# Layer norm, memory-recurrent attention and a squared-ReLU feed-forward layer on one core: loads put in another order, feed-forward slots and stores moved

## The chip, the cores and the metric

The kernel runs on one core of one Trainium2 chip. The core has TensorE (PE; its weight loads are shown apart as PEld), VectorE (DVE), ScalarE (ACT), GpSimd (POOL) and SyncE (SP, which issues DMAs), and 16 DMA engines that all issuing queues share. The metric is the device time of one execution in microseconds (us), the median of several runs. A profile shows one execution; its span goes from the first instruction to the last.

## What is computed

The input is 2048 rows of width 640. `A` is a recurrent attention: 64 segments of 32 rows, each with 8 memory rows in front; the first 8 output rows of one segment are the memory of the next, so the 64 steps run one after the other. `B` is a feed-forward layer of width 1728.

```python
# A: per segment, h = [mem (8 rows); layernorm(x)[segment] (32 rows)]
q, k, v = h @ Wq, h @ Wk, h @ Wv              # 32 heads of 128
p = softmax(where(mask, q @ k.T * 128**-0.5, -1e9))
o = (p @ v) @ Wo                              # 40 rows of 640
mem, out_rows = o[:8], o[8:]                  # mem goes to the next segment
# whole
h  = x + A(layernorm(x))
h2 = h + relu(layernorm(h) @ w1 + b1)**2 @ w2 + b2
```

## The kernel before

All tensors are bf16 and sums are f32 in PSUM. The q, k, v weights (`wq`, `wk`, `wv`: 5 chunks of 128 rows by 4096 columns each) and `wo` (32 heads of 128 by 640) stay in SBUF. Since the width is cut into 4 groups of 160 = 128 + 32, the fifth chunk of each weight is gathered from 4 blocks of 32 rows: a DMA from DRAM to DRAM collects them in `w4s` (called the relay here, issued by ACT) and a second DMA brings them in.

Work goes in 16 batches of 128 rows, each of 4 steps (one step is one segment; `step`, L396). A step multiplies the 8 memory rows and the first 24 rows of its segment by `wq`, `wk`, `wv` (each two halves of 20 matmuls, `half`, `pass_units`), turns q and k by transposes (`turn`), makes scores (`pss`), exponentials, sums (`pz`), the product with v (`po`), and the output projection `pw` of 128 small matmuls. `wo_out` casts it to `o`; `mem_to_hT` turns the first 8 rows of `o` into the memory of the next step. The last 8 rows of each segment (tail) don't feed the memory, so they are computed for the four segments of a batch together: `tail_units` spreads their q, k, v passes, `wo_tail_units` their projection (`psw`) over the steps of the batch before or after. Every step stores 24 rows of `o` to `a_rows` in DRAM (4 DMAs, L501), the tail of a batch another 16 DMAs (L276).

The feed-forward layer of batch b-1 runs inside the steps of batch b, one slot (`ff_slot`) at two places a step: the first after the k passes (tag `pv3`), the second behind `pz` (tag `pv0`). A slot p of 8 does two blocks of w1 (`psf`, 10 matmuls), the two blocks of w2 that belong to slot p-1 (`acc`, 4 matmuls), and ACT's relu and POOL's square for the next. After its matmuls each slot issues on SP the loads of w1 for slot p+1 and w2 for slot p (`ff_load1`, `ff_load2`: two DMAs each, single-buffered `w1c`, `w2c`); w1 is read from `w1d`, a copy of w1 in DRAM that POOL's queue lays out after batch 0 (L589, L591). Before slot 0 come `ff_rows` (reload of x and `a_rows`), `ff_stats` (sum, mean, variance; inverse root by Newton steps on POOL in `ln_root`), `ff_apply` (`hn`) and `ff_turn` (transposes `pth`, `hnT`).

In the last step `last_loads` brings the whole of w1 and w2 into the place of `wq` (`fw`); after the last step come the tail projection of batch 15, the rest of batch 14's slots and the whole feed-forward layer of batch 15.

The order on PE, ACT, DVE and POOL is that of the program (`manual_schedule`); SP is left to the scheduler. The lists in `sl` hold what is put at a place of a step: q (after the q passes), k (after the k passes), v, d (after the second slot), w0 (before `wo_out`), w (end). `pre` and `mid` are the units ahead of and behind `po`, `post` those around `mem_to_hT`.

Of the kernel before, what the change touches and what calls it, by code (L numbers as in the profile page):

```python
# [18 lines left out]
def kernel(  # L19
# [55 lines left out]
    w1d = dram.tile([FC, 128, DC, 128], BF16)  # L75
# [44 lines left out]

    def ln_apply(dst, src, mv, rstd):
        nc.vector.tensor_scalar(out=dst, in0=src, scalar1=mv[:, 0:1], scalar2=rstd[:],  # L122
                                op0=ALU.subtract, op1=ALU.mult)
# [7 lines left out]
    with tc.tile_pool(name="wts", bufs=1) as wts, tc.tile_pool(name="s1", bufs=1) as s1, \  # L131
            tc.tile_pool(name="s2", bufs=2) as s2, tc.tile_pool(name="s4", bufs=4) as s4, \
# [11 lines left out]
        def load_x(b):  # L144
            xt = s1.tile([128, D], BF16, tag="xt", name="xt")
# [8 lines left out]
        for wi, src in enumerate((A_Wq, A_Wk, A_Wv)):  # L154
            nc.scalar.dma_start(out=w4s[wi].rearrange("(g r) f -> g r f", g=G),
                                in_=src.rearrange("(g q) h e -> g q (h e)", g=G)[:, 128:DG, :])
        for wi, (w, src) in enumerate(((wq, A_Wq), (wk, A_Wk), (wv, A_Wv))):
            w2d = src.rearrange("d h e -> d (h e)")
            for c in range(4):
                nc.sync.dma_start(out=w[:, c, :], in_=w2d[c * DG:c * DG + 128, :])  # L160
            nc.sync.dma_start(out=w[:, 4, :], in_=w4s[wi])
        wov = A_Wo.rearrange("h e d -> e h d")
        for j in range(4):
            (nc.sync if j % 2 else nc.scalar).dma_start(out=wo[:, j * 8:(j + 1) * 8, :], in_=wov[:, j * 8:(j + 1) * 8, :])
# [6 lines left out]
        nc.vector.tensor_copy(out=b1f[:], in_=b1b[:])  # L171
# [6 lines left out]
        def ln_b(b):  # L178
# [4 lines left out]
            roots[b] = (mv, ln_root(s1, mv))  # L183
# [77 lines left out]

        def wo_tail_units(b):
# [3 lines left out]
            def unit(k):  # L266
                def f():
# [3 lines left out]
                    if k == 7:  # L271
                        ot = wo_out(st["ps"])
                        for g in range(G):
                            for sp in range(4):
                                r0 = b * 128 + sp * SEG + HD
                                nc.sync.dma_start(out=a_rows[r0:r0 + TL, g * DG:(g + 1) * DG],  # L276
                                                  in_=ot[32 * g + sp * TL:32 * g + (sp + 1) * TL, :])
# [17 lines left out]

        def ff_load1(p):
            for fc in (2 * p, 2 * p + 1):
                if room:
                    w1q.append(room["w1"][:, :, fc * 128:fc * 128 + fs_of(fc)])
                    continue  # L300
                t = s2.tile([128, DC, 128], BF16, tag="w1c", name="w1c")
                nc.sync.dma_start(out=t[:, :, 0:fs_of(fc)], in_=w1d[fc][:, :, 0:fs_of(fc)])
                w1q.append(t)

        def ff_load2(p):
            for fc in (2 * p, 2 * p + 1):
                if room:
                    w2q.append(room["w2"][:, fc, :])
                    continue
                t = s2.tile([128, D], BF16, tag="w2c", name="w2c")  # L310
                fs = fs_of(fc)
                nc.sync.dma_start(out=t[0:fs], in_=B_w2[fc * 128:fc * 128 + fs, :])
                if fs < 128:
                    nc.sync.dma_start(out=t[fs:fs + 1], in_=B_b2.rearrange("(o d) -> o d", o=1))
                w2q.append(t)

        def ff_rows(b):
# [3 lines left out]
            nc.sync.dma_start(out=a_[:], in_=a_rows[b * 128:(b + 1) * 128, :])  # L321
            fst[b] = {"a": a_, "h": h_}

        def ff_stats(b):
# [3 lines left out]
            nc.vector.tensor_tensor(out=f["h"][:], in0=f["a"][:], in1=f["h"][:], op=ALU.add)  # L328
            for j in range(2):
                ln_stats(st, j, f["h"])  # L330
            nc.vector.bn_aggr(out=mv[:], in_=st[:])
            f["mv"], f["r"] = mv, ln_root(s1, mv)
# [15 lines left out]
        def ff_slot(b, p, tag):  # L348
            f = fst[b]
            f1 = []  # L350
            if p < NP:
                ps = psum_v.tile([128, 4, 128], F32, tag=tag, name="psf")
                for j in range(2):
                    fc = 2 * p + j
                    fs = fs_of(fc)
                    w1c = w1q.pop(0)
                    for c in range(DC):
                        nc.tensor.matmul(ps[0:fs, j, :], lhsT=w1c[:, c, 0:fs], rhs=f["hnT"][:, c, :], start=(c == 0),  # L358
                                         stop=(c == DC - 1))
                ff_load1((p + 1) % NP)  # L360
            if p > 0:
                for j in range(2):
# [3 lines left out]
                    w2c = w2q.pop(0)  # L366
                    for hf in range(2):
                        if fc == 0:
                            f["acc", hf] = psum_v.tile([128, 512], F32, tag="acc%d" % hf, name="acc%d" % hf)
                        nc.tensor.matmul(f["acc", hf][:, 0:320], lhsT=t1[0:k, :], rhs=w2c[0:k, hf * 320:(hf + 1) * 320],  # L370
                                         start=(fc == 0), stop=(fc == FC - 1))
            if p < NP:
                ff_load2(p)
                for j in range(2):
# [3 lines left out]
                    t1 = s4.tile([128, 128], BF16, tag="f1", name="f1")  # L378
# [7 lines left out]
            if p == NP:  # L386
# [6 lines left out]
                run_ff(tag)  # L393

        ffq = []

        def run_ff(tag):
            if ffq:
                ffq.pop(0)(tag)

        def step(s, first, pre, mid, post, slots):
# [21 lines left out]
            run(first[2])  # L423
            run(slots.get("k", ()))
            run_ff("pv3")
            turn(qr, qT[:, :, :, 0:SEG], "act", psum_v, "pv0")
            turn(kr, kT[:], "dve", psum_v, "pv1")
            pv = [psum.tile([128, 512], F32, tag="mm", name="ps%d" % n) for n in range(1)]
# [42 lines left out]
            run_ff("pv0")  # L471
# [166 lines left out]
```

## Time and profile before

| what | us |
|---|---|
| median of 5 runs (1294.22 to 1300.98) | 1297.53 |
| the profiled execution | 1297.53 |
| its span, first to last instruction | 1295.5 |
| mean granted TensorE clock, as a share | 0.981 |
| DMA: 112.55 MB in 97577 packets, mean | 87 GB/s |

In a row of a timeline stand the start, the time taken, engine, line, operation, out<-in, shapes and the count; in brackets the idle time of the engine before it and what ended it. "issue" means that nothing in the profile shows what the engine waited for. A row that stands for several instructions has their common span. A row of waits has the engine and line, what was waited for, us in total, how often, and the longest.

### The profile page before, as it was taken

The numbers are of one execution on the slowest core, as the hardware profiler recorded it, in microseconds if no ns is written. First come the engines' busy times: TensorE is split into PE (matmuls) and PEld (weight loads), VectorE is DVE, ScalarE is ACT, GpSimd is POOL, SyncE is SP. The second block draws the span as 40 slices with busy tenths as digits, with TensorE's granted clock in tenths as the row PEclk, the third lists the DMA queues.
The fourth block names the chain that finished last, engine by engine and source line by source line (L and its number), as shares of the span: only waits on it lengthen the run. The fifth ranks groups of instructions, "written<-read, shape, count | busy, mean of one in ns | idle before, by whom it ended". The sixth has DMA issues, their size and how long they took to land. (4 is left out here: it accounts for less than half of the span.)

```text
span 1295.5 us, 68304 instructions
## 1 busy us (share of the span) xinstructions
PE 1085.8 (84%) x31488; PEld 707.8 (55%) x31488; DVE 464.4 (36%) x987; ACT 414.2 (32%) x848; POOL 304.4 (23%) x981
## 2 busy tenths in 40 slices
PE   0057878999999999989999899899998999899865
PEld 0025545656566665656565565656565665656553
DVE  0003333344343434344433434343433434343411
ACT  0012323334333333333333333333333333333312
POOL 3001132222222222222222222222222222222213
PEclk9999989999999999999999999999999999999977
DMA  7840031223223232223222232223222232222250
GB/s 302 329 151 5 6 94 31 77 77 91 63 66 89 75 86 63 78 71 91 68 78 72 76 91 60 71 76 92 77 71 68 77 92 71 61 68 86 77 182 17
DMA packets 97577, 112.55 MB, mean 87 GB/s; under 512 B 30732, under 2 KB 94123, under 8 KB 95323
## 3 DMA queue, kind: packets, MB, share of 16 engines
q1 hardware_dynamic: 94078, 100.19, 25.2%
q8 instruction: 246, 4.03, 1.2%
q10 hardware_dynamic: 2140, 5.77, 1.2%
q0 software_dynamic: 1072, 2.23, 0.6%
q14 instruction: 41, 0.33, 0.1%
HBM read 102.88 MB, written 10.60 MB: 88 GB/s over the span
## 5 line engine op out<-in xcount | busy, mean ns | idle before, releaser
L208 PEld LDWEIGHTS <-hT 128*32 128x32 bf16 x7680 | 205.3, 97 | 183.3 <-DVE hT L287 7.9
L227 PE MATMUL pw<-wo,oT 128*32 128x160 bf16 x8192 | 167.5, 237 | 45.9 <-issue 42.4
L227 PEld LDWEIGHTS <-oT 128*32 128x32 bf16 x8192 | 148.1, 99 | 69.4 <-issue 50.5
L208 PE MATMUL ps<-wv,hT 128*32 128x512 bf16 x2560 | 163.5, 383 | 0.0
L381 POOL TENSOR_TENSOR f<-ffr 128x128 bf16<-128x128 bf16 x224 | 84.3, 396 | 327.0 <-ACT ffr L379 275.5
L208 PE MATMUL ps<-wq,hT 128*32 128x512 bf16 x2560 | 153.3, 385 | 6.4 <-DVE hT L287 6.2
L208 PE MATMUL ps<-wk,hT 128*32 128x512 bf16 x2560 | 149.8, 379 | 0.0
L129 DVE CAST vr<-ps 128x512 bf16<-128x512 f32 x128 | 88.5, 692 | 72.1 <-PE ps L208 68.7
L379 ACT ACTIVATE ffr<-psf,b1f 128x128 bf16<-128x128 f32 x224 | 68.9, 358 | 91.8 <-PE psf L358 90.0
L129 DVE CAST qr<-ps 128x512 bf16<-128x512 f32 x64 | 44.3, 692 | 139.8 <-PE ps L208 139.8
L232 DVE CAST o<-pw 128x160 bf16<-128x160 f32 x64 | 20.8, 325 | 183.0 <-PE pw L227 179.5
L127 ACT COPY qT<-pt 128x1024 bf16<-128x1024 bf16 x64 | 64.8, 1012 | 58.2 <-PE pt L220 58.2
L358 PE MATMUL psf<-hnT,w1c 128*128 128x128 bf16 (+1 forms) x1020 | 76.0, 220 | 8.6 <-DMA w1c<-w1d 8.6
L451 POOL TENSOR_TENSOR p<-p,mask_t 128x128 bf16<-128x128 bf16 x64 | 27.4, 429 | 223.8 <-ACT p L444 223.8
L129 DVE CAST oT<-po 128x320 bf16<-128x320 f32 x128 | 56.9, 486 | 64.2 <-PE po L486 54.0
L127 ACT CAST qr<-ps 128x512 bf16<-128x512 f32 x64 | 37.5, 586 | 122.1 <-PE ps L208 122.1
L127 ACT CAST tq<-pst 128x512 bf16<-128x512 f32 x32 | 19.0, 592 | 176.9 <-PE pst L208 176.9
L358 PEld LDWEIGHTS <-w1c 128*128 128x128 bf16 (+1 forms) x1020 | 60.6, 99 | 25.5 <-issue 11.5
L370 PE MATMUL acc<-w2c,f 128*128 128x320 bf16 x404 | 72.6, 301 | 1.9 <-DMA w2c<-in_B_w_dram 1.9
L127 ACT CAST oT<-po 128x320 bf16<-128x320 f32 x128 | 48.2, 429 | 68.7 <-PE po L486 68.7
L127 ACT CAST kr<-ps 128x512 bf16<-128x512 f32 x64 | 37.5, 586 | 100.3 <-PE ps L208 100.3
L467 POOL TENSOR_TENSOR pn<-p,rk 128x128 bf16<-128x128 bf16 x64 | 42.7, 667 | 107.1 <-issue 80.8
(97 smaller groups left out, 1373.9 us busy)
## 6 DMA issues: line engine op xcount, KB each, us to landing
w1c<-w1d SPq DMA_DIRECT2D x190, 160.0 KB
w2c<-in_B_w_dram SPq DMA_DIRECT2D x188, 160.0 KB
wq<-in_A_Wq_dram SPq DMA_DIRECT2D x4, 1024.0 KB
wk<-in_A_Wk_dram SPq DMA_DIRECT2D x4, 1024.0 KB
wv<-in_A_Wv_dram SPq DMA_DIRECT2D x4, 1024.0 KB
a_rows<-o SPq DMA_DIRECT2D x256, 7.5 KB
a_rows<-o SPq DMA_DIRECT2D x256, 2.5 KB
xt<-in_A_x_dram SPq DMA_DIRECT2D x16, 160.0 KB
```

Of the source, the lines that this page charges most:

```text
L127: nc.scalar.copy(out=out_, in_=in_)
L129: nc.vector.tensor_copy(out=out_, in_=in_)
L208: nc.tensor.matmul(ps[32 * g:32 * g + 32, :], lhsT=lhs(c), rhs=w[:, c, g * EG + n * 512:g * EG + (n + 1) * 512], start=(c == 0), stop=(c = ...
L227: nc.tensor.matmul(ps[32 * g:32 * g + 32, 0:DG], lhsT=lhs(h), rhs=wo[:, h, g * DG:(g + 1) * DG], start=(h == 0), stop=(h == H - 1))
L232: nc.vector.tensor_copy(out=o[:], in_=ps[:, 0:DG])
L358: nc.tensor.matmul(ps[0:fs, j, :], lhsT=w1c[:, c, 0:fs], rhs=f["hnT"][:, c, :], start=(c == 0), stop=(c == DC - 1))
L370: nc.tensor.matmul(f["acc", hf][:, 0:320], lhsT=t1[0:k, :], rhs=w2c[0:k, hf * 320:(hf + 1) * 320], start=(fc == 0), stop=(fc == FC - 1))
L379: nc.scalar.activation(out=r[0:fs], in_=ps[0:fs, j, :], func=ACT.Relu, bias=b1f[0:fs, fc:fc + 1], scale=1.0)
L381: nc.gpsimd.tensor_tensor(out=t1[0:fs], in0=r[0:fs], in1=r[0:fs], op=ALU.mult)
L451: nc.gpsimd.tensor_tensor(out=p[:, :, NQ:NC], in0=p[:, :, NQ:NC], in1=mask_t[:, sp].unsqueeze(1).to_broadcast([128, HG, M + TL]), op=ALU.mult)
L467: nc.gpsimd.tensor_tensor(out=pn[:, :, NQ:NC].rearrange("p i (a q) -> p i a q", q=M), in0=p[:, :, NQ:NC].rearrange("p i (a q) -> p i a q", ...
```

## The change

- The start: SP is put under the program's order as well. The relays go from ACT's queue to SP's, one ahead of each weight, with 16 rows as the outermost dimension in place of 4 groups; all of `wo` goes to SP; the second batch's x is loaded at the start into another buffer; the first two inverse roots are made on ACT (`ln_root_act`: logarithm, then exponential); the cast of the bias `b1f` moves to batch 1. In step 0 the first v tail passes stand behind the turns.
- w1's copy in DRAM is laid out by pairs of blocks, `[FC // 2, 128, DC, 256]`, one DMA on SP in each of steps 0 to 6. A slot then has one DMA for w1 and one for w2.
- The loads of a slot are put in a list `later`. Those of the first slot go out at once, those of the second (`hold`) behind the first store of `o`, or at the end of the step's stores.
- The 16 tail stores are queued and issued in two lots of 8: behind the stores of step 0 of a batch, and at v of step 1. `ff_rows` moves to d of step 1.
- `ff_apply` moves to k of step 2, `ff_turn` to a new place f ahead of `mem_to_hT` in step 2, and the 8 slots to steps 3, 0, 1, 2. The last slot no longer calls the next item.
- The end: `last_loads` stands after the first slot, loads pairs in the order of use, and builds a selection matrix `sel`. The last rows of batch 15 no longer go through `a_rows`: eight matmuls with `sel` put them into PSUM (`pa`) and `ff_stats` adds them. Its statistics come ahead of batch 14's last slots, and the roots of batches 14 and 15 are made on ACT.
- `f1` has three buffers in place of four.

```diff
-    w1d = dram.tile([FC, 128, DC, 128], BF16)
+    w1d = dram.tile([FC // 2, 128, DC, 256], BF16)
...
+    def ln_root_act(pool, mv):
+        rstd = pool.tile([128, 1], F32, tag="lnrs", name="lnrs")
+        nc.scalar.activation(out=rstd[:], in_=mv[:, 1:2], func=ACT.Ln, bias=eps_t[:])
+        nc.scalar.activation(out=rstd[:], in_=rstd[:], func=ACT.Exp, scale=-0.5)
+        return rstd
...
-                                                        mybir.EngineType.DVE, mybir.EngineType.Pool}))
+                                                        mybir.EngineType.DVE, mybir.EngineType.Pool,
+                                                        mybir.EngineType.SP}))
...
         load_x(0)
+        load_x(1)
...
-        for wi, src in enumerate((A_Wq, A_Wk, A_Wv)):
-            nc.scalar.dma_start(out=w4s[wi].rearrange("(g r) f -> g r f", g=G),
-                                in_=src.rearrange("(g q) h e -> g q (h e)", g=G)[:, 128:DG, :])
+        def relay(wi):
+            nc.sync.dma_start(out=w4s[wi].rearrange("(g r t) f -> r g t f", g=G, t=2),
+                              in_=(A_Wq, A_Wk, A_Wv)[wi].rearrange("(g q) h e -> g q (h e)", g=G)[
+                                  :, 128:DG, :].rearrange("g (r t) f -> r g t f", t=2))
+
+        relay(0)
         for wi, (w, src) in enumerate(((wq, A_Wq), (wk, A_Wk), (wv, A_Wv))):
             w2d = src.rearrange("d h e -> d (h e)")
             for c in range(4):
                 nc.sync.dma_start(out=w[:, c, :], in_=w2d[c * DG:c * DG + 128, :])
+            if wi < 2:
+                relay(wi + 1)
             nc.sync.dma_start(out=w[:, 4, :], in_=w4s[wi])
...
+        def run_stores(n, engs=(nc.sync,)):
+            for j in range(n):
+                stores.pop(0)(engs[j % len(engs)])
...
-                ff_load1((p + 1) % NP)
+                if p + 1 < NP or b + 2 < NB:
+                    later.append(lambda: ff_load1((p + 1) % NP))
...
-                ff_load2(p)
+                if p > 0 or b == 0 or True:
+                    later.append(lambda: ff_load2(p))
...
+        def run_ff(tag, hold=False):
             if ffq:
                 ffq.pop(0)(tag)
+            if not hold:
+                run_later()
+
+        def run_later():
+            while later:
+                later.pop(0)()
...
-            run_ff("pv0")
+            run_ff("pv0", hold=True)
...
-            for g in range(G):
-                nc.sync.dma_start(out=a_rows[s * SEG:s * SEG + HD, g * DG:(g + 1) * DG],
-                                  in_=o[32 * g + M:32 * g + SEG, :])
+            if s + 1 == 4 * NB:
+                fst["o"] = o
+            else:
+                for g in range(G):
+                    nc.sync.dma_start(out=a_rows[s * SEG:s * SEG + HD, g * DG:(g + 1) * DG],
+                                      in_=o[32 * g + M:32 * g + SEG, :])
+                    if g == 0:
+                        run_later()
+            run_later()
+            run(slots.get("s", ()))
             run(post[0])
+            run(slots.get("f", ()))
...
+            for k in range(NP):
+                p1, p2 = (k + 3) % NP, (k + 2) % NP
+                nc.sync.dma_start(out=whole[1, p1][:, :, 0:width(p1)], in_=w1d[p1][:, :, 0:width(p1)])
+                load2(whole[2, p2], p2)
...
+                if b > 0 and nxt:
                     if sp == 1:
-                        sl["q"].append(lambda b=b: ff_rows(b - 1))
+                        sl["v"].append(lambda: run_stores(8))
+                        sl["d"].append(lambda b=b: ff_rows(b - 1))
...
                     if sp == 2:
+                        sl["k"].append(lambda b=b: ff_apply(b - 1))
+                        sl["f"] = [lambda b=b: ff_turn(b - 1)]
+                    if sp == 3:
+                        ffq.extend(lambda tag, b=b, p=p: ff_slot(b - 1, p, tag) for p in range(NP + 1))
...
+        run_later()
         room.update(whole)
         for f in wo_tail_units(NB - 1):
             f()
-        ff_rows(NB - 1)
...
+        run_ff("pv0")
+        pa = [psum_v.tile([128, 512], F32, tag="pv%d" % (1 + hf), name="pa%d" % hf) for hf in range(2)]
+        for k, src in ((1, fst.pop("o")), (0, fst.pop("ot"))):
+            for g in range(G):
+                nc.tensor.matmul(pa[g // 2][:, g % 2 * DG:(g % 2 + 1) * DG], lhsT=fst["sel"][:, k, g, :],
+                                 rhs=src[:], start=(k == 1 and g % 2 == 0), stop=(k == 0), skip_group_check=True)
+        ff_stats(NB - 1, True, pa)
         ff_apply(NB - 1)
+        while ffq:
+            run_ff(("pv3", "pv0")[len(ffq) % 2])
         ff_turn(NB - 1)
+        ff_load1(0)
         for p in range(NP + 1):
-            ff_slot(NB - 1, p, tags[p % 2])
+            ff_slot(NB - 1, p, ("pv3", "pv0")[p % 2])
+            run_later()
```

More of the change, by code (lines that the diff above doesn't have):

```diff
@@ L163 @@
         for j in range(4):
[L164 removed]
+            nc.sync.dma_start(out=wo[:, j * 8:(j + 1) * 8, :], in_=wov[:, j * 8:(j + 1) * 8, :])
         b1b = const.tile([128, FC], BF16)
@@ L328, in ff_stats @@
             nc.vector.tensor_tensor(out=f["h"][:], in0=f["a"][:], in1=f["h"][:], op=ALU.add)
+            for hf, ps in enumerate(more):
+                cs = slice(hf * 320, (hf + 1) * 320)
+                nc.vector.tensor_tensor(out=f["h"][:, cs], in0=ps[:, 0:320], in1=f["h"][:, cs], op=ALU.add)
             for j in range(2):
@@ L512 @@
         ln_transpose(0)
-        load_x(1)
         mem_to_hT(o0, hT4s[0], 0)
```

153 lines of the change are left out of this document (90 added, 63 removed).

## The prediction

> **What bounds the kernel now.** I read the page first, then who waited for whom on TensorE in three stretches (start-up, the steady batches, the end), then the timelines of the stretches where it waited.
>
> ```profile
> PE 1085.8 (84%) x31488; PEld 707.8 (55%) x31488; DVE 464.4 (36%) x987; ACT 414.2 (32%) x848; POOL 304.4 (23%) x981
> ```
>
> PE is busy 1085.8 of 1295.5 us and nothing else is above 36%, so the question is only what PE waits for. Its waits from 0 to 158 us, from 226 to 1230 us, and from 1230 us on (engine, what it waited for, us in total, times, longest):
>
> ```profile
> PE ptx L196 <- DVE xn L122: 57.8, 2, 33.3
> PE pst L208 <- DMA wq<-w4s: 17.6, 1, 17.6
> ```
> ```profile
> PE pw L227 <- issue: 38.7, 35, 2.0
> PE psw L227 <- issue: 8.4, 7, 2.0
> PE po L480 <- DVE pn L466: 7.9, 15, 1.1
> PE pth L343 <- DVE hn L122: 7.9, 13, 0.8
> PE pm L283 <- DVE o L232: 6.4, 15, 0.4
> ```
> ```profile
> PE pth L343 <- DVE hn L122: 9.9, 1, 9.9
> PE psf L358 <- DMA w1c<-w1d: 8.6, 1, 8.6
> ```
>
> Three places, then: about 75 us in which PE waits for the first weights, some 47 us spread over the output projections with no releaser that the profile shows, and two holes of about 9 us at the end. The work PE does is nearly the same after the change, so the sum is made of holes that close.
>
> **1. Start-up: x, the relays (`w4s`), the weights.** Timeline rows of the start, two windows (PE, PEld, DVE, ACT, POOL busy, granted clock, DMA share, GB/s) and the sizes of the loads:
>
> ```profile
> 0.84 1.22 ACTq L155 DMA_DIRECT2D w4s<-in_A_Wq_dram  x1
> ...
> 49.36 0.60 ACTq L155 DMA_DIRECT2D w4s<-in_A_Wk_dram  x1
> ...
> 78.77 2.75 PE L208 MATMUL pst<-wq,hTt 128*32 128x512 bf16 x24 [17.58 <-DMA wq<-w4s]
> ...
> 94.75 2.33 PE L208 MATMUL pst<-wv,hTt 128*32 128x512 bf16 x40
> ...
> 107.42 0.33 DVE L232 CAST o<-pw 128x160 bf16<-128x160 f32 x1 [2.88 <-PE pw L227]
> ```
> ```profile
> 12.00:16.00 4.00, 0.00 (x0) 0.00 (x0) 0.00 (x0) 0.00 (x0) 0.00 (x0) 1.00 0.28 111
> 20.00:44.00 24.00, 0.87 (x10) 0.67 (x10) 1.45 (x6) 0.00 (x0) 2.70 (x14) 1.00 1.01 417
> ```
> ```profile
> wq<-in_A_Wq_dram SPq DMA_DIRECT2D x4, 1024.0 KB
> wo<-in_A_Wo_dram SPq DMA_DIRECT2D x2, 1280.0 KB
> ```
>
> The DMA engines can move 417 GB/s, yet `wq` is whole only at 78.77, because its last fifth passes through the relay and that first relay holds its queue until 49.36. In 12 to 16 us the DMA share is 0.28, about 4 of 16 engines: the old relay has the 4 groups as its outermost dimension. After the change one queue carries, in the order of use, x twice, relay, `wq`, relay, `wk`, relay, `wv`, `wo`; each relay has 16 outermost. What must be in before step 0 can end is 15 x 1024 KB of q, k, v, 3 x 1024 KB of relays, 4 x 1280 KB of `wo` and 320 KB of x: 24.4 MB, 58.6 us at 417 GB/s. With 1 us to the first issue, 1.5 us of ramp and 2 us until the last piece is seen (estimates), `wo` is whole at 63 us. The other bound is PE: `wv` is in after 19.2 MB, at about 51 us, and from the start of its tail passes to the end of `o` the rows give 107.75 - 94.75 = 13.0 us, so 64 us. Either way the first `o` is out at about 65 us in place of 107.75: **42 us**. Bounds: 34 if a relay, which reads and writes DRAM, costs twice its bytes (7.5 us more); 46 if neither ramp nor clock costs anything. The first two normalisations (ACT in place of POOL, second x up front, the `b1f` cast out of DVE's way) cost nothing and bring nothing of their own: they end near 15 us, under the wait for `wq` at about 23 us. Without that cover they would cost their own few us.
>
> **2. The w1 relay on POOL after batch 0.** Two rows of POOL's timeline, and TensorE's waits from 158 to 226 us:
>
> ```profile
> 162.55 1.25 POOL L589 DMA_DIRECT2D w1d<-in_B_w_dram  x1
> ...
> 170.96 0.41 POOL L416 COPY qT<-qTt 128x256 bf16<-128x256 bf16 x1
> ```
> ```profile
> PE pss L437 <- POOL qT L416: 5.5, 1, 5.5
> PE pw L227 <- issue: 2.8, 3, 1.3
> ...
> PE psw L227 <- issue: 0.7, 1, 0.7
> ```
>
> Ten DMA issues hold POOL from 162.55 to 170.96, the copy of step 4 stands behind them, and PE waits 5.5 us, long enough to come back slow. On SP, one DMA a step in steps 0 to 6, behind the stores, nothing waits for it. **7 us**, between 5 (the wait alone) and 9.
>
> **3. The weight loads of the second slot, and stores.** The instruction queue on the page, TensorE's wait in batch 0 (0 to 158 us), then one step with such loads and the step before it, which loads no w2 there: rows of SP, two windows, rows of PE.
>
> ```profile
> q8 instruction: 246, 4.03, 1.2%
> ```
> ```profile
> PE pw L227 <- issue: 0.9, 2, 0.6
> ```
> ```profile
> 734.97 0.80 SPq L302 DMA_DIRECT2D w1c<-w1d  x2
> 735.88 0.85 SPq L312 DMA_DIRECT2D w2c<-in_B_w_dram  x2
> ```
> ```profile
> 736.00:738.00 2.00, 1.99 (x112) 1.39 (x113) 1.72 (x4) 0.91 (x3) 1.17 (x3) 1.00 0.95 298
> 739.00:741.00 2.00, 0.56 (x33) 0.36 (x25) 0.00 (x0) 0.00 (x0) 0.00 (x0) 1.00 0.00 0
> ```
> ```profile
> 721.42 2.40 PE L227 MATMUL pw<-wo,oT 128*32 128x160 bf16 x128
> ...
> 737.46 1.82 PE L227 MATMUL pw<-wo,oT 128*32 128x160 bf16 x93
> 740.73 0.80 PE L227 MATMUL pw<-wo,oT 128*32 128x160 bf16 x35 [1.44 <-issue]
> ```
>
> The projection runs 128 matmuls and 128 weight loads in 2.40 us, the densest stretch of PE's stream. The instruction queue q8 moved 4.03 MB in 246 packets, 16.4 KB each, and its count fits PE's 62,976 instructions at 256 a packet. I read the 1.44 us as PE having run out of instructions because a packet was held up by the burst of weights (share 0.95) just before. All engines are idle at 739 to 741 and so is DMA, so it is no data wait. The change takes that burst away from there: w1 and w2 of the second slot now go out behind the first store of `o`, and land while the q and k passes run, which ask for 160 instructions in 4.4 us. The burst was over within 4.0 us of its first issue (734.97, idle by 739). From the end of `o` to the next first slot lie two passes and the turn of the memory rows, about 5 us, of which a store's issue takes 0.4: about 0.6 us to spare.
>
> How much of 38.7 + 8.4 us goes is the largest unknown. All of it, 47, if the burst is the whole cause. None, if a packet's own time against 2.40 us is. Steps without such loads tell: steps 0 to 6 lost 0.9 + 2.8 + 0.7 = 4.4 us, 0.63 a step; the 55 steps from 226 to 1230 us lost 47.1, 0.86 a step. The burst adds 0.23 a step to a stall that the alignment of the stream makes anyway: over 57 steps **13 us**, and that I take.
>
> The Trainium skill, "Runtime: NRT & Kernel Launch", section "Instruction fetch mechanics", speaks against even that: it holds that 16 KiB blocks are fetched ahead and that crossing into the next is mostly hidden; by it this term would be 0 and the sum 13 us smaller. The packet size agrees with q8's 16.4 KB; the 1.44 us with DMA idle does not.
>
> Stores of a batch's tail rows (16 of them) move to two places further on, SP time only. In step 1 of a batch the reload `ffa` now stands behind the last eight: eight issues, then a wait until they have landed. Behind it on SP wait the stores of `o`, and on DVE the first add of the statistics heads the next step's evacuations. In the order of the queue I estimate it in about 3 us before its use, so nothing.
>
> **4. The transposes of the normalised rows.** In step 2 of each batch PE waits for `hn` (7.9 us over 13) and at `pm` for `o` (6.4 us over 15, 0.43 each). The change puts `hn` after the cast of `kr` and the transposes into the 0.43 us hole. It gains the 7.9 and about 0.3 x 14 of transposes, and pays about 0.1 us a batch since `hnT` goes ahead of `hT` on DVE. **11 us**, between 8 and 14. `f1` with three buffers and the final adds beside the second slot's ACT work cost nothing; cover is the `po` wait.
>
> **5. The end.** Timeline rows; step 63, the last, starts at 1233.72.
>
> ```profile
> 1233.72 1.48 PE L208 MATMUL ps<-wq,hT 128*32 128x512 bf16 x24 [0.31 <-DVE hT L287]
> ...
> 1236.11 2.25 SPq L524 DMA_DIRECT2D fw<-in_B_w_dram  x5
> ...
> 1252.15 1.25 PE L358 MATMUL psf<-hnT,w1c 128*128 128x128 bf16 x10 [8.64 <-DMA w1c<-w1d]
> ...
> 1255.62 4.46 PE L227 MATMUL pw<-wo,oT 128*32 128x160 bf16 x128 [0.54 <-ACT oT L127]
> ...
> 1269.03 0.89 DVE L390 TENSOR_TENSOR ffh<-acc,ffh 128x320 bf16<-128x320 f32 x2 [5.81 <-PE acc L370]
> ...
> 1280.28 2.31 PE L358 MATMUL psf<-hnT,fw 128*128 128x128 bf16 x20 [0.59 <-DVE hnT L129]
> ```
>
> What can go: 8.6 us for `w1c` stuck behind the whole weights, 2.1 us of a slow projection (4.46 against 2.40), about 1 us of like slowness elsewhere (2.31 for the 20 matmuls at 1280.28), and 11.2 us from the last `acc` to 1280.28. That is 23 us. What comes: eight matmuls that add the last rows straight from SBUF (1 us). Slot 3 of batch 14, whose weights are still asked for behind the whole loads: the old ones took 16.0 us from 1236.11 to 1252.15, the new start about 6 us into step 63, so in at 22; PE is there at 18, which is 4 us of wait. Then ACT: logarithm and exponential of the last root stand ahead of the relus of slots 4 to 7 and wait for DVE's sums, which makes 2.5 us of hole. Net **15 us**, between 9 and 19.
>
> **Sum.** 42 + 7 + 13 + 11 + 15 = 88 us from the profiled execution, 1297.5 us around a span of 1295.5, which is also the median of the runs: **1209 us**.
>
> **Rivals.** (a) The projections keep their stalls: a packet's own time sets them, or they are no fetch at all. For it: the stalls of steps 0 to 6. Against: the burst just before the 1.44 us. 1209 + 13 = 1222 us. The second reading is what the section of the Trainium skill named above would have. (b) They go altogether, 47 in place of 13: 1175 us. For: the clean 2.40 us of the step without w2. (c) The relay still runs on four rings. Then each of those carries 0.79 MB beside its sixteenth of 21.3 MB, 2.1 MB at 26 GB/s, 81 us, and `wo` is in at 85: 20 us lost, 1229 us. Against: 0.28 of 16 engines fits the outermost 4, which is now 16. (d) Slower: SP's order is now the program's, and a held load that lands late stops PE in the first slot of every step. With 0.6 us to spare, landings 2.2 us later than now cost 1.6 us in each of 56 steps and eat the 88; 3 us later give 1209 + 134 = 1343 us. Against: half as many load issues on SP, and a DMA that idles between bursts.
>
> **How the numbers follow.** Forecast 0.58, (a) 0.17, (b) 0.10, (c) 0.08, (d) 0.03, and 0.04 that little of the big pieces shows. About 0.3% is what a measurement can tell from no change here: faster 0.95, same 0.02, slower 0.03. The bounds of the terms alone give 1175 to 1230 if two or three of them fall the same way; with (a) and (c) above and most of (b) below, the range is 1179 to 1235.
>
> **What would show it.** First `o` near 65 us with `wq` first used near 23; no wait of `pss` on POOL in step 4; "issue" before `pw` and `psw` near 38 us in place of 51; no `pth` wait in step 2; from step 63's start to the end 47 us in place of 62. Wrong if the first `o` is after 75, if waits for `w1c` or `w2c` appear in the steady steps, or if DVE's add waits for `ffa`.

## The result, and the profile after

The changed kernel takes **1219.28 us** (median of 9 runs, 1214.4 to 1222.45), the kernel before 1298.04 in the same series (16 runs): a ratio of 0.9395, 95% interval 0.9378 to 0.9412. The forecast was 1209 us with a range of 1179 to 1235: inside the range, 10 us too fast. The profiled execution took 1218.23 us around a span of 1216.5 at a mean granted clock of 0.983.

Two lines of the page: the engines, and the instruction queue.

```profile
PE 1089.2 (90%) x31496; PEld 711.6 (58%) x31496; DVE 466.6 (38%) x991; ACT 416.9 (34%) x856; POOL 288.4 (24%) x924
q8 instruction: 246, 4.03, 1.3%
```

PE does the same work as before (1085.8 us) in a span 79 us shorter: as forecast, the whole gain is holes that closed. Where they were can be read off the first matmul at `pm` of each step, which ends the step before. The first and the last such row of TensorE's timeline, of the kernel before and then of the one after (the table is worked out from all of them):

```profile
107.80 0.19 PE L283 MATMUL pm<-ident,o 128*128 128x32 bf16 x1 [0.42 <-DVE o L232]
...
1233.10 0.19 PE L283 MATMUL pm<-ident,o 128*128 128x32 bf16 x1 [0.43 <-DVE o L232]
```
```profile
70.56 0.21 PE L306 MATMUL pm<-ident,o 128*128 128x32 bf16 x1 [0.43 <-DVE o L247]
...
1164.41 0.19 PE L306 MATMUL pm<-ident,o 128*128 128x32 bf16 x1 [0.44 <-DVE o L247]
```

| stretch | before, us | after, us | gain | forecast |
|---|---|---|---|---|
| step 0, from the start to its end | 107.8 | 70.6 | 37.2 | 42 |
| steps 1 to 3 | 49.7 | 50.6 | -0.9 | 0 |
| step 4 | 26.4 | 19.9 | 6.6 | 7 |
| steps 5 to 62 | 1049.2 | 1023.4 | 25.8 | 13 + 11 |
| from there to the end | 62.4 | 52.1 | 10.3 | 15 |

The gains add up to the 79 us. The start and the end each gave 5 us less than forecast, the rest is within 2 us. TensorE's waits in steps 5 to 62 (engine, what it waited for, us in total, times, longest), before and after:

```profile
PE pw L227 <- issue: 40.2, 37, 2.0
PE po L480 <- DVE pn L466: 9.5, 17, 1.1
PE pth L343 <- DVE hn L122: 9.1, 14, 1.3
PE psw L227 <- issue: 8.4, 7, 2.0
PE pm L283 <- DVE o L232: 6.9, 16, 0.4
```
```profile
PE pw L242 <- issue: 31.8, 37, 1.4
PE psw L242 <- issue: 6.0, 7, 1.2
PE ps L223 <- DVE hT L310: 5.5, 16, 0.6
PE po L527 <- DVE pn L513: 5.4, 14, 1.1
PE acc L410 <- DMA w2c<-in_B_w_dram: 3.3, 7, 0.9
...
PE pm L306 <- DVE o L247: 1.5, 2, 1.1
```

All rows of these two views sum to 86.1 and 59.4 us: 26.7 of waits went, and the steps became 25.8 us shorter. The stalls without a releaser ahead of `pw` and `psw` fell by 10.8, the waits for `hn` by 9.1, those for `o` by 5.4 and those for `pn` by 4.1; the waits for `w2c` grew by 1.4 (1.9 before).

The start after the change, TensorE's timeline and windows (PE, PEld, DVE, ACT, POOL busy, granted clock, DMA share, GB/s):

```profile
25.75 2.75 PE L223 MATMUL pst<-wq,hTt 128*32 128x512 bf16 x24 [4.39 <-DMA wq<-w4s]
...
68.87 1.26 PE L242 MATMUL pw<-wo,oT 128*32 128x160 bf16 x32 [2.21 <-DMA wo<-in_A_Wo_dram]
```
```profile
0.00:4.00 4.00, 0.00 (x0) 0.00 (x0) 1.48 (x12) 1.28 (x1) 3.35 (x21) 1.00 0.31 85
4.00:8.00 4.00, 0.87 (x10) 0.67 (x10) 2.60 (x10) 0.54 (x3) 4.00 (x7) 1.00 0.86 268
16.00:20.00 4.00, 1.24 (x8) 0.22 (x8) 0.00 (x0) 0.00 (x0) 0.00 (x0) 1.00 1.05 438
60.00:64.00 4.00, 1.85 (x113) 1.65 (x115) 1.38 (x3) 0.82 (x3) 1.12 (x3) 0.95 1.06 361
```

The DMA engines are now busy from 8 to 64 us (shares of 0.97 to 1.09 in windows of 4 us), and PE waits for each weight as it comes: the start is bound by the loads. The end, from the last `pw` on, and two windows, the first of the kernel before while its last `pw` runs, the second of the one after:

```profile
1179.10 3.75 PE L242 MATMUL pw<-wo,oT 128*32 128x160 bf16 x122 [0.50 <-ACT oT L136]
1185.15 0.32 PE L242 MATMUL pw<-wo,oT 128*32 128x160 bf16 x6 [2.31 <-issue]
1185.24 2.31 PE L242 MATMUL psw<-wo,oTt 128*32 128x160 bf16 x122
1189.99 0.45 PE L242 MATMUL psw<-wo,oTt 128*32 128x160 bf16 x6 [2.44 <-issue]
1191.57 1.25 PE L397 MATMUL psf<-hnT,w1c 128*128 128x128 bf16 x10 [1.12 <-DMA w1c<-w1d]
```

```profile
1256.00:1258.00 2.00, 2.00 (x70) 2.00 (x66) 0.13 (x1) 0.00 (x0) 0.40 (x1) 0.50 0.17 56
```
```profile
1180.00:1182.00 2.00, 2.00 (x72) 2.00 (x65) 0.00 (x0) 0.00 (x0) 0.14 (x1) 0.50 1.13 314
```

Here two stalls of 2.3 and 2.4 us stand where the forecast had none. Between them lie 6 + 122 = 128 matmuls, with their weight loads 256 instructions. And the projection itself is still slow, 3.75 us for 122 matmuls, at a granted clock of 0.50; the clock was 0.50 too while the 128 of the kernel before took 4.46 us.

### The profile page after: what moved, and what is told of

It is laid out like the page before. It is cut to its first block, busy times and chain, and to the rows that moved or that the text cites. A ratio compares the mean times of both kernels' runs of the same rounds, so it can differ in the third digit from the quotient of the medians.

```text
span 1216.5 us, 67900 instructions
## 1 busy us (share of the span) xinstructions
PE 1089.2 (90%) x31496; PEld 711.6 (58%) x31496; DVE 466.6 (38%) x991; ACT 416.9 (34%) x856; POOL 288.4 (24%) x924
## 3 DMA queue, kind: packets, MB, share of 16 engines
q8 instruction: 246, 4.03, 1.3%
## 4 chain that ended last, share of the span: by engine, by line
PE 74%; DMA 10%; issue 5%; DVE 4%; ACT 3%; SPq 2%; POOL 1%; POOLq 0%; DVEq 0%; ACTq 0%
PE ps L223 30%; PE pw L242 13%; PE pst L223 7%; PE pt L235 5%; DMA w2c<-in_B_w_dram 5%; PE psf L397 4%; PE acc L410 4%; PE psw L242 3%; DMA w4s<-in_A_Wv_dram 2%; PE po L527 2%; PE po L533 2%; PE pz L504 1%; SPq L180 1%; PE pss L488 1%; DVE pn L513 1%
## 5 line engine op out<-in xcount | busy, mean ns | idle before, releaser
L242 PE MATMUL pw<-wo,oT 128*32 128x160 bf16 x8192 | 169.2, 239 | 42.7 <-issue 35.5
L138 DVE CAST kr<-ps 128x512 bf16<-128x512 f32 x64 | 44.3, 692 | 76.2 <-PE ps L223 75.9
L223 PEld LDWEIGHTS <-hTt 128*32 128x32 bf16 x1920 | 41.2, 96 | 55.0 <-issue 38.4
```

What stands on the lines that cost most here:

```text
L138: nc.vector.tensor_copy(out=out_, in_=in_)
L223: nc.tensor.matmul(ps[32 * g:32 * g + 32, :], lhsT=lhs(c), rhs=w[:, c, g * EG + n * 512:g * EG + (n + 1) * 512], start=(c == 0), stop=(c = ...
L242: nc.tensor.matmul(ps[32 * g:32 * g + 32, 0:DG], lhsT=lhs(h), rhs=wo[:, h, g * DG:(g + 1) * DG], start=(h == 0), stop=(h == H - 1))
```

## The experiments

Each is the changed kernel with one edit. The difference is that of its ratio to the one of the changed kernel (0.9395), times 1298 us; with intervals of 0.2 to 0.4% on either side, differences under 4 to 5 us are not told apart. Single profiles can't settle them either: steps 5 to 62 took 1023.4 us in the changed kernel and 1022.5 to 1029.7 in seven runs below that change nothing there. By these runs the 25.8 us gained in those steps may be 20 to 27.

### What the start is worth: relays on four rings, no relays, another queue

`relay4`:
```diff
-            nc.sync.dma_start(out=w4s[wi].rearrange("(g r t) f -> r g t f", g=G, t=2), ...
+            nc.sync.dma_start(out=w4s[wi].rearrange("(g r) f -> g r f", g=G), ...
```


> The relays keep their new queue and their new place in the order, but run with the 4 groups as the outermost dimension, as before the change. Ring theory (the outermost dimension decides how many of the 16 engines take part, 0.28 of them in the profile before): 0.79 MB of each relay sit on each of 4 engines, about 15 us a relay hidden only in part: the first pm at about 90 us in place of 70.6 and 1239 us. Order theory (the new order alone brings the start's 37 us): within 3 us of 1219.

Measured 1240.17 us, ratio 0.9541 (0.9504 to 0.9578): 19 us slower. Its start, in rows of TensorE's timeline and waits:

```profile
89.77 0.21 PE L305 MATMUL pm<-ident,o 128*128 128x32 bf16 x1 [0.43 <-DVE o L246]
```
```profile
PE pst L222 <- DMA wk<-w4s: 11.7, 1, 11.7
PE pst L222 <- DMA wq<-w4s: 11.4, 1, 11.4
```

The first `pm` at 89.8 for 90 expected: of the start's 37 us the new outermost dimension is worth 19. The other 18 belong to the rest of the change to the start, the new queue and order among it; no run takes them apart.

`direct`, and `directact` with the same loads on ACT's queue:
```diff
-            if wi < 2:
-                relay(wi + 1)
-            nc.sync.dma_start(out=w[:, 4, :], in_=w4s[wi])
+            for g in range(G):
+                nc.sync.dma_start(out=w[32 * g:32 * g + 32, 4, :], in_=w2d[g * DG + 128:(g + 1) * DG, :])
```


> No relay: the fifth chunk of wq, wk and wv is read by four DMAs of 32 rows each, straight from the weights. Theory (the start is bound by the bytes that the DMA engines move): the 3 x 1024 KB of the relays fall away, 3.1 MB, 7.5 us at 417 GB/s: the first pm at 63 us in place of 70.6, and 1212 us. Rival 1 (the PE work behind wv sets the start): within 2 us of 1219. Rival 2 (a DMA over 32 partitions runs on fewer of the 16 engines): 12 such DMAs of 256 KB at a quarter of the rate, about 104 GB/s, cost 7.6 us each weight in place of 4.9 for relay and load, the first pm later by up to 8 us, 1227.

> As the run without relays, but its twelve loads over 32 partitions go out on ACT's queue at the start, beside the loads over 128 partitions on SP's. In the run without relays the DMA share stayed at 1.0 while 191 to 252 GB/s were moved in the stretches of the small loads. If a stretch is slow since all 16 engines then write to the same 32 partitions, mixing them with other loads brings the rate back to about 417 GB/s: 21.3 MB, the first pm at about 63 us in place of 70.6 to 71.9, 1212 us. If each such packet takes an engine twice as long whatever goes beside it, the first pm stays near 71 and the time at 1219 to 1221 us. ACT's first evacuations may stand behind the issues: up to 5 us later at the first weight, hidden by the waits for the next.

`direct` took 1220.38 us (0.9399, 0.9373 to 0.9426), `directact` 1221.9 (0.9424, 0.9395 to 0.9453): no gain from 3.1 MB less. Windows of `direct` in which the small loads move, then one of `directact` while both kinds are in flight:

```profile
16.00:20.00 4.00, 0.62 (x4) 0.11 (x3) 0.00 (x0) 0.00 (x0) 0.00 (x0) 1.00 1.07 252
...
48.00:52.00 4.00, 2.29 (x36) 1.22 (x29) 1.38 (x2) 1.01 (x1) 0.00 (x0) 1.00 0.98 191
```
```profile
12.00:16.00 4.00, 0.00 (x0) 0.00 (x0) 0.00 (x0) 0.00 (x0) 0.00 (x0) 1.00 1.11 221
```

All engines are busy and half as much moves: 3.1 MB at about 210 GB/s take 15 us, and the 6.3 MB of the three relays (out and in) at 417 take 15 too. That is why nothing was gained. Mixing with wide loads doesn't help; the mix runs at 221 as well. The Trainium skill has a rule for this in "SBUF — State Buffer", section "Door 1: The DMA port swizzle": a transfer's rate depends on how many of 16 ports its partitions reach, and a block of 32 partitions reaches 8. The halved rates agree with it. `directact` had a loss of its own besides: ACT's first root stood behind the issues on its queue, and the first `pm` came at 74.6 us (71.9 in `direct`).

### The w1 relay on POOL

```diff
-                if s < NP:
-                    sl["s"] = sl.get("s", []) + [lambda p=s: nc.sync.dma_start(out=w1d[p, ...
+            if b == 0:
+                for p in range(NP):
+                    nc.gpsimd.dma_start(out=w1d[p, ...
```


> The copy of w1 by pairs goes out on POOL's queue after batch 0, as before the change (7 issues there in place of 10), in place of one issue on SP in each of steps 0 to 6. Theory: POOL's copy of qT in step 4 stands behind the issues and pss waits for it: 0.7 of the 6.6 us that step 4 gained come back, 4 to 6 us, 1224 us; the trace shows pss waiting for POOL in step 4. Rival (the gain of step 4 came from something else): no such wait, 1219 us.

Measured 1228.56 us, 0.9449 (0.9413 to 0.9484): 7 us slower. A row of TensorE's waits in step 4, and two rows of POOL:

```profile
PE pss L484 <- POOL qT L462: 3.3, 1, 3.3
```
```profile
126.87 5.90 POOL L671 DMA_DIRECT2D w1d<-in_B_w_dram  x7
131.51 1.66 POOL L462 COPY qT<-qTt 128x256 bf16<-128x256 bf16 x1
```

The copy waits behind the issues as before, and step 4 takes 25.8 us in place of 19.9. Of these 6 us 3.3 are the wait; behind it the granted clock was 0.58 from 132 to 136 us, where it was 1.00 all through step 4 of the changed kernel. The reading of that term holds.

### What the held loads are worth

```diff
-            run_ff("pv0", hold=True)
+            run_ff("pv0")
```


> The loads of the second slot go out at once again, as before the change; all else is the changed kernel. Burst theory (the loads landing while the output projection runs lengthen its stalls, 0.23 us a step over 57 steps): 13 us come back, the time is about 1232 us, and TensorE's waits with no releaser ahead of pw and psw rise from 45.6 us to about 58. Alignment rival (the stalls are made by the stream alone): within 3 us of 1219, stalls near 46 us. Between them: the two profiles differ by 51.5 - 45.6 = 6 us in these stalls, so 1225 us would say that the burst is real and half the size.

Measured 1246.05 us, 0.961 (0.9576 to 0.9645): 28 us slower, twice what the burst theory gave. TensorE's waits in steps 5 to 62:

```profile
PE pw L242 <- issue: 44.6, 35, 2.3
PE psw L242 <- issue: 11.8, 7, 2.7
```

The stalls are 56.4 us there: 18.6 more than with the loads held, and 7.8 more than **before the change** (48.6). The other 10 us are a slower TensorE: it is busy for 969.1 us there in place of 958.7, for the same matmuls. Its granted clock stood at 0.50 in seven stretches, 27 us together, against one of 3.4 us in the changed kernel and two in the kernel before. Six of the seven begin within 1.2 us of the end of a stall of 1.96 to 2.55 us; three other stalls of 2.07 to 2.72 us have none behind them.

So the burst is real, and the rest of the change had made it worse. What did so was not taken apart; a likely part is that the reload of `ffh` and `ffa` now stands at the same place of step 1 as the two weight loads.

What the stalls are is seen by counting. In one step of the changed kernel (TensorE, then a window):

```profile
559.55 1.56 PE L242 MATMUL psw<-wo,oTt 128*32 128x160 bf16 x79
561.96 0.24 PE L242 MATMUL psw<-wo,oTt 128*32 128x160 bf16 x1 [0.85 <-issue]
561.96 2.39 PE L242 MATMUL pw<-wo,oT 128*32 128x160 bf16 x127
565.70 0.24 PE L242 MATMUL pw<-wo,oT 128*32 128x160 bf16 x1 [1.35 <-issue]
```
```profile
563.00:565.70 2.70, 1.36 (x80) 1.15 (x68) 0.00 (x0) 0.00 (x0) 0.06 (x1) 1.00 0.03 6
```

From stall to stall there are again 1 + 127 = 128 matmuls, 256 instructions, the size of a q8 packet (4.03 MB in 246 packets, 256 of PE's 62,992 instructions each), and DMA is idle. Counted through the whole trace, 61 of the gaps of over 0.35 us from the start of one PE instruction to that of the next stand at eight neighbouring places of the count by 256 (192 to 199), 60 of them at the very same one; no other eight places together have more than 10. In the kernel before 57 stand at that place. Blocks of 256 between step 5 and 62, by the time in which PE worked off their instructions, with the mean gap behind them, the mean time from block to block, and how many had a DMA share of 0.3 or more in the last 2.5 us (worked out from the start of every PE instruction):

```
worked off in     changed kernel                  loads not held
                  blocks  gap   period  with DMA  blocks  gap   period  with DMA
under 2.6 us          50  0.99  3.21    7             45  1.37  3.58    34
2.6 to 3.0 us         10  0.71  3.45    1              9  1.09  3.83     5
3.0 to 3.4 us         10  0.14  3.32    0              9  0.35  3.54     3
over 3.4 us          151  0.11  5.26   63            152  0.11  5.21    53
```

A block worked off in under 2.6 us is followed by the next 3.2 us after its own start on average, 3.6 where the loads are not held; blocks of over 3.4 us lose next to nothing. These are means and no floor: in the changed kernel single blocks were followed after 2.2 to 3.8 us, a third of them in under 3.0. After two blocks that had taken 12 us or more together it was 2.8 us on average, after two of under 10 us 3.4. The 128 matmuls of `pw` and their weight loads are one such block, worked off in 2.4 us. So most of the stall, about 0.8 us a block, is there without any load, and the burst adds some 0.4.

### Fewer instructions in the projection

```diff
-            wo_units(lambda h: oT[:, h, 0:SEG], pw, 0, H)
+            for h in range(0, H, 2):
+                for g in range(G):
+                    nc.tensor.matmul(pw[32 * g:32 * g + 32, 0:DG], lhsT=oT[:, h, 0:SEG], ...
```


> The output projection pw of every step takes every other head only: 64 matmuls in place of 128 (half of the sum is left out, so the output is another). Block theory: TensorE's instructions come in blocks of 256 (16 KB each), and from the start of one block to that of the next at least 3.2 us pass; a stall is what 3.2 us exceed the time in which the block's instructions were worked off. Going through the changed kernel's instructions from step 5 to 62 with that rule gives 53 us of stalls there (the profile shows 60 at these places), and 28 with half of pw left out. So the time falls by the work, 64 x 1.2 = 77 us, and by 25 us of stalls: 1117 us, and the waits with no releaser ahead of pw and psw fall from 45.6 to about 22 us. Rival (the stalls come with the step, from its DMA or from PE's hand-over between tiles, whatever the number of instructions): they stay near 45 us, and the time falls by 77 us only, to 1142.

Measured 1123.34 us, 0.8635 (0.8596 to 0.8674): 96 to 99 us less, for 102 by the block theory and 77 by the rival. The waits:

```profile
PE pw L546 <- issue: 11.2, 9, 2.9
PE psw L242 <- issue: 10.8, 9, 1.9
...
PE psf L397 <- DMA w1c<-w1d: 3.6, 1, 3.6
```

11.2 + 10.8 = 22.0 us of stalls, the 22 expected. PE now gets to slot 3 of the end sooner and waits 3.6 us for `w1c` in place of 1.1: 2.5 of the 3 to 6 us that are missing to 102.

### The same instructions, spread

`spread` puts units of the tail passes from ahead of `pw` between its parts, `spread2` two that stood behind it:
```diff
-            run(mid)
+            run(mid[:len(mid) - inner])
...
-            wo_units(lambda h: oT[:, h, 0:SEG], pw, 0, H)
+            for k in range(inner + 1):
+                wo_units(lambda h: oT[:, h, 0:SEG], pw, at[k], at[k + 1])
+                run(mid[len(mid) - inner + k:][:1] if k < inner else ())
```
```diff
-            wo_units(lambda h: oT[:, h, 0:SEG], pw, 0, H)
+            at = (0, 16, 24, H) if sp < 2 else (0, 12, 22, H)
+            for k in range(3):
+                wo_units(lambda h: oT[:, h, 0:SEG], pw, at[k], at[k + 1])
+                run(slots.get("i", ())[k:k + 1])
```


> In steps 1, 2 and 3 of a batch the units of the tail passes (4 matmuls of 512 columns each) that stood ahead of the output projection are put between its parts, 10 or 16 heads apart; the work is the same, in another order. Instruction theory (PE consumes 256 instructions of 128 matmuls and 128 weight loads in 2.4 us, faster than a 16 KB packet of the instruction queue follows): the stalls of steps 1 to 3, 0.60, 0.36 and 0.49 us a step over 14 batches, shrink by about two thirds, 13 us in all: 1206 us, with step 0 of a batch unchanged at 2.1 us. Rival (the stalls come from the DMA burst or from something in the projection itself, not from its density): 1219 us, or slower where o is now late for pm.

> The density of the output projection again, this time without touching what stands ahead of it: in steps 0, 1 and 3 of a batch two units of the tail passes that stood behind the projection are put inside it (after heads 16 and 24, in step 3 after 12 and 22). Instruction theory: 256 instructions then take 4.1 us in place of 2.4, and of the stalls before pw (steps 0, 1, 3 of a batch: 2.08, 0.60 and 0.49 us with those of psw) about 0.9, 0.3 and 0.3 go, as the run with units taken from ahead of the projection showed 0.25 in steps 1 and 3; over 14 batches 21 us, at most: 1198 us; no new waits for oT (13.7 us there). It is less where o is now late for pm or the held loads, which go out 1.7 us later against their use, for the first slot: up to 1 us in 42 steps, 1219 or more. Rival (the stalls follow the DMA alone): 1219 us.

Both miss: 1228.3 us (0.9459, 0.9433 to 0.9485) and 1223.18 (0.9439, 0.9415 to 0.9464). The stalls fell in the first (29.6 + 8.3 us in place of 35.5 + 10.1 over the whole run), hardly in the second (32.1 + 11.3), and each lost more in a wait that grew, `spread` for `oT` (3.4 us in the changed kernel) and `spread2` for `o` (3.2):

```profile
PE pw L242 <- ACT oT L136: 13.7, 48, 0.6
```
```profile
PE pm L306 <- DVE o L247: 9.6, 33, 1.3
```

The price of a unit was wrong (the second expectation has 4.1 us in place of 2.4 for two units, 0.85 each): a unit's four matmuls run side by side and it adds some 0.2 us, as in these rows of `spread2` (508.99 to 509.20):

```profile
508.99 0.39 PE L223 MATMUL pst<-wk,hTt 128*32 128x512 bf16 x4
509.20 0.59 PE L242 MATMUL pw<-wo,oT 128*32 128x160 bf16 x24
```

Two units stretch the block by 0.4 us, not by 1.7, and a unit covers as little. The runs thus don't speak against the block theory, and don't prove it either; they show that this filler is too thin, and that units ahead of and behind `pw` are needed as cover.

### The transposes of the normalised rows

```diff
-                        sl["k"].append(lambda b=b: ff_apply(b - 1))
-                        sl["f"] = [lambda b=b: ff_turn(b - 1)]
+                        sl["q"].append(lambda b=b: ff_apply(b - 1))
+                        sl["a"] = [lambda b=b: ff_turn(b - 1)]
```


> In step 2 of a batch the normalised rows are applied after the q passes and turned right behind the first slot, as before the change; the slots stay where the change put them. Theory: PE waits for hn again in every batch (0.6 us, 7.9 in all) and at pm for o again (0.2 us more), with about 0.1 us a batch given back: 11 us slower, 1230 us. Rival (the gain of the steady steps is that of the slots' new places and of the last slot's adds, not of the transposes): within 3 us of 1219.

Measured 1224.86 us, 0.9434 (0.9409 to 0.9459): 5 us slower, half of the expected. Steps 5 to 62:

```profile
PE pm L306 <- DVE o L247: 7.3, 17, 0.4
...
PE pth L382 <- DVE hn L131: 1.3, 1, 1.3
```

The wait for `o` is back (1.5 in the changed kernel), the one for `hn` is not, but for one in the last batches: slot 6 now stands ahead of the turns and covers it. So of the two waits, that for `o` went by the transposes' new place, that for `hn` by the slots' new places.

### The end

`fw3` moves `room.update(whole)` into `last_loads`, `lateloads` loads five of the seven pairs later, `endq` does the first and loads two pairs earlier:
```diff
+            room.update(whole)
...
-        room.update(whole)
```
```diff
-            for k in range(NP):
+            whole_load(0, 2)
...
+        whole_load(2, NP)
```
```diff
+                    sl["q"].append(lambda: whole_load(0, 2))
                     sl["a"] = [last_loads]
```


> Slot 3 of batch 14 reads its w1 and w2 from the whole weights, which bring these two first, in place of loads of its own that were still issued behind them. Theory: 0.65 MB less in the burst and no wait of psf for w1c (1.1 us): 1 to 2 us off the end, 1217 to 1218 us. Rival: the wait is hidden by the next one (hnT, the slow projections), 1219 us.

> Of the seven pairs of w1 and w2 that are loaded in the last step the first two stay at their place, the other five go out behind the tail projection of the last batch, so that the burst no longer falls on the two projections of the end. Theory (the burst makes the stalls of 2.3 us before pw and 2.4 us before psw at the end): they fall to about 0.6 each and the end is 3 us shorter, 1216 us, if the 3.3 MB that are late (9 us at 370 GB/s) still land ahead of their slots; if not, a wait for fw of up to 5 us stands ahead of slots 4 to 7 and the time is 1219 to 1222 us. Rival (these stalls are made by the stream alone): the stalls stay at 4.7 us together, 1219 us or more.

> The whole weights of the last step go out in two lots, the first two pairs right behind the q passes and the other five behind the first slot, and slot 3 of batch 14 reads from them in place of loads of its own. 5.2 MB at 370 GB/s from 1168 us on are in by about 1182, when the last pw begins. Theory (a block of instructions that is fetched beside such a burst comes 1.5 to 2 us later): the stalls of 2.3 and 2.4 us before the last pw and psw fall to about 0.6 each, the 1.1 us wait for w1c goes: 4 us less, 1215 us. Rival (the burst only moves: slot 2 or po of the last step are late in place of it, or the loads of slot 2, now behind two pairs, come late): 1219 us.

Measured 1219.18 us (0.9405, 0.937 to 0.9439), 1216.54 (0.938, 0.9353 to 0.9408) and 1217.89 (0.9373, 0.9342 to 0.9403): none is told apart from the changed kernel. In the profiles, the stretch from the last step's first `pm` to the end takes 52.3, 48.5 and 48.6 us for 52.1. The two stalls in `lateloads`, and in `endq`:

```profile
1185.89 0.32 PE L242 MATMUL pw<-wo,oT 128*32 128x160 bf16 x6 [0.44 <-issue]
...
1191.00 0.32 PE L242 MATMUL psw<-wo,oTt 128*32 128x160 bf16 x6 [2.72 <-issue]
```
```profile
1190.46 0.32 PE L242 MATMUL pw<-wo,oT 128*32 128x160 bf16 x6 [0.72 <-issue]
...
1194.48 0.32 PE L242 MATMUL psw<-wo,oTt 128*32 128x160 bf16 x6 [1.62 <-issue]
```

In `lateloads` the later five pairs did not wait for `psw`, as I had meant, but only behind the reload of `ffa`, which waits 6.6 us on SP for DVE's clearing of that tile, itself behind the casts of `oT`; so the burst missed `pw` (0.44) and fell on `psw` (2.72). `pw` also ran at a granted clock of 1.00 there: 2.32 us for its 122 matmuls in place of 3.75. In `endq` the burst is nearly over before `psw` (0.39 of the DMA share, 124 GB/s, from 1190 to 1194 us), and both are shorter than 2.31 and 2.44 us. `fw3` lost its wait for `w1c`, but the next wait, for `f`, was 1.5 us in place of 0.4. About 3.5 us are to be had here by the profiles; a version clearly faster than the changed kernel was not found.

## Why the prediction was right, and where it was off

The total alone doesn't tell the forecast from rival (a): 1219 lies 10 us from 1209 and 3 from (a)'s 1222. The stretches do.

1. **The start, 42 forecast, 37.2 measured.** Relay, queue and order work as read, and 16 outermost against 4 is worth 19 of it. The rate was over-sized. The first `o` is out at 70.2 us in place of 65, since `wo` is whole at 68.9 and not at 63. In the first 8 us, 1.4 MB move (85 and 268 GB/s), 4.6 us lost where 2.5 were allowed; the 5.2 MB of `wo` run at 361 to 365 GB/s in place of 417, 1.9 us more. These are 4 of the 6 us.
2. **The w1 relay, 7 forecast, 6.6 measured**; put back, 6.0 us return to step 4, the wait and the slow clock behind it, as the prediction read them.
3. **The held loads, 13 forecast, 10.8 us of stalls gone** in steps 5 to 62. The size is right for a reason that was half right. The base of the stall, which I laid to "the alignment of the stream", is that a dense block of 256 instructions takes 3.2 us on average; the burst adds some 0.4 to it. With the loads held, 37.8 us over 58 steps are left, 0.65 a step, for the 0.63 read from steps 0 to 6. But the rest of the change added 7.8 us of stalls and the hold took away 18.6, and with them 10 us of a slower TensorE, which the term didn't have; that only the net is near the forecast is luck. By the prediction's own mark, the stalls of the whole run, it missed: 45.6 us for 38 forecast (51.5 before), since 4.8 new ones stand at the end. The rule of the Trainium skill cited in the prediction ("Runtime: NRT & Kernel Launch", "Instruction fetch mechanics"), that crossing a block is mostly hidden, doesn't hold for a stretch this dense: 45.6 us of the changed kernel's span go there.
4. **The transposes, 11 forecast**, 9.1 (`hn`) and 5.4 (`o`) of waits gone, less 0.6 more for `hT`: 14, within what else moved. The mechanism is half right: by `turnback` the transposes' new place is worth 5 us, and the wait for `hn` went by the slots' new places, which the term didn't count on. The wait for `pn`, 4.1 us less, was not forecast at all.
5. **The end, 15 forecast, 10.3 measured.** The step that failed is that the slow projections would go (2.1 us) with nothing in their place. From the start of `pw` to the end of `psw` they took 7.2 us before (1255.62 to 1262.84) and 11.3 after (1179.10 to 1190.44). The whole weights still burst beside them, now at 1174 to 1190 us, with 2.31 + 2.44 us of stalls at the block boundaries, and `pw` again ran at a granted clock of 0.50, which the prediction had not looked at. `endq` and `lateloads` won 3.5 us back in their profiles: in `lateloads` 1.6 of it are shorter stalls and 1.4 a `pw` at full clock. Two terms were over-sized the other way and hid part of the miss: the wait for `w1c`, forecast at 4, was 1.1, and of the 2.5 us laid to ACT, for which the prediction showed no row, the waits for `f` in slots 4 to 7 show 0.9.

Rival (c), a relay still on four rings, was priced at 1229 us; it did not come, and `relay4`, which brings it about, took 1240. (d) did not come, though its mark shows faintly: 3.3 us of waits for `w2c` in the steady steps, where they were to show if the held loads were late, against 1.9 before. DVE's first add, another sign named there, never waited for `ffa` in these steps. (a) has its mechanism in part, since a packet's own time is the larger part of a stall, but 10.8 us of the steady stalls did go; (b) falls because 37.8 us stay with the loads held.

## What to carry to other kernels

Where PE waits for nothing that the profile shows, count the instructions between two such waits: if they are always 256, the stretch is too dense for its instructions. Fewer instructions helped here; slower blocks lost next to nothing, but no run made a dense one slow enough. Large transfers beside such a stretch make it worse and are better put beside sparse ones. Where a matmul row takes longer than its like, look at the granted clock before laying it to the loads beside it. A gather over 32 partitions can cost as much as a detour over all 128 although it moves half the bytes. And before a unit of work is used as filler or cover, take its price from a row in which it runs without waits.

## What the runs showed of the hardware

- TensorE's instructions come in blocks of 256, one q8 packet each. Blocks worked off in under 2.6 us follow each other 3.2 us apart on average (2.2 to 3.8), 3.6 where loads are not held; a boundary costs 0.85 and 1.35 us in the dense stretch shown with idle DMA, 2.3 to 2.7 beside the burst at the end, and next to nothing behind blocks that take over 3.4 us.
- Behind six of the nine stalls of 1.96 us or more in steps 5 to 62 of `nohold`, within 1.2 us of their end, a stretch of 3.4 or 6.8 us at a granted clock of 0.50 began.
- Loads over 32 partitions moved at 191 to 252 GB/s with all 16 engines busy, loads over 128 partitions with 8 KB rows at 403 to 438, `wo` with its rows of 1280 bytes at 361 to 365.
- A copy between DRAM tensors with an outermost dimension of 4 holds its weight back by 11.4 to 11.7 us against 4.4 to 4.5 with 16.
